# Bucketed attention and a two-layer MLP on one core: the values of batch 0 loaded once, an offset column built on TensorE, and a new table of keys

## The chip, the cores and the metric

One core of one Trainium2 chip runs the whole program; a core has TensorE (PE), VectorE (DVE), ScalarE (ACT), GpSimd (POOL) and the queue engine SyncE (SP). The metric is device microseconds of one execution, lower is better.

## The reference

Attention over four batches, eight heads, 768 rows and a head size of 64. A row of q and a row of k see each other only if six hash bits agree, the signs of their products with `proj`. The attention output, heads side by side, goes through a GELU layer pair of 512 to 2048 to 512.

```python
q_bits = (np.einsum('bhsd,dk->bhsk', q, proj) > 0)      # six bits; k likewise
mask = q_bucket[:, :, :, None] == k_bucket[:, :, None, :]
scores = np.where(mask, scale * np.matmul(q, k.transpose(0, 1, 3, 2)), -1e9)
attn = np.exp(scores - np.max(scores, axis=-1, keepdims=True))
attn = attn / (np.sum(attn, axis=-1, keepdims=True) + 1e-09)
x = np.matmul(attn, v)          # heads side by side: [3072, 512]
h = x @ w_in                    # [3072, 2048]
out = (0.5 * h * (1.0 + erf(h / sqrt(2)))) @ w_out
```

The inputs are float32. On the host the kernel's call lays q and k out as one array `qk` (128 rows by 768 per head: q above k), v as [768, 512] per batch, the weights as pairs of 32-bit words (they are decoded on the chip), and `offset`, a column of 128 numbers, in which rows 0 to 5 hold a tiny negative and rows 6 to 11 a tiny positive number, and rows 64 to 75 the same.

## The kernel before

**What runs.** The work is cut into 192 *units*: one block of 128 query rows of one head against all 768 keys. A unit (`unit`, line 892) is a score product into a PSUM tile `s` (line 908, or 910 and 911), a row maximum on DVE (L914), three small steps, an exponential on ACT (L928), a reciprocal (L937) and a division. Then the 128 by 768 probabilities are turned: in batch 0 by six PE transposes into PSUM (L987) with two copies back (tile `pt`), in the later batches by a DMA transpose after a split into two float16 halves. `values` (line 1016) multiplies them with v: L1031 with float32 values (batch 0 and the batch after it), L1040 with halves. The result `x` feeds the hidden layer (L1249), its evacuation and GELU on ACT, a split on DVE, and the output layer (L1331).

**Batch 0** is cut into two passes (`FIRST`): all eight heads for rows 0 to 255 (16 units), then all eight for the other 512 (32 units). Its heads are *plain* in the first pass (`head_plain`, line 842): q and k are loaded as they are (two loads of 64 by 768 each, L849), four small products give the hash values (L861), ACT takes their signs with `off` as bias (L866), and four copies write masks beside q and k. The bias settles the sign of a hash value of exactly zero. All other heads go through `head` (line 562): one load of 128 by 768 (`raw`, L572), its maximum on DVE (L575), a scale by way of a small product (`head_scale`, L532), a split into halves with copies and moves, hash products (L640) and signs with the bias `off16` (L646).

**Set-up** (`set_up`, line 472). `off` is loaded in four pieces on ACT's queue (L370). `off16`, which holds the column in another arrangement, is cleared (L493) and then loaded in eight small pieces on SP's queue (`offsets`, line 486, issued at L490).

**Values of batch 0.** `v_scale` (line 776) finds the largest magnitude of v: four loads of 128 by 6 by 128, one per pair of heads (L784), four maxima (L789), and a few small steps for a scale that `x` needs (L1061). For batch 0 these loads land in the buffers `wraw`, which afterwards receive the weights. The product reads v from elsewhere: `values_whole` (line 811) loads the same pieces again into the buffers `vhl` (L813), four in the first pass and four in the second.

**What sets the order.** Nothing is issued by hand. Each piece of work is a `Step` with an engine (or several that may do it), a cost and a key; `Plan.order` (line 119) goes through them as events, gives each free engine the ready step with the lowest key plus a shift for the engine, and the program is then written in that order. Every engine runs its own list strictly in that order. The keys come from the table `PAR` and the unit's number. 64 *blank* steps of four products each (L389, key 5000) fill PE wherever the planner sees nothing else to run there. Transfers from HBM all go out on SP in the planner's order.

**Weights.** Each of the 32 loads (L690, three `wraw` buffers) is decoded by three DVE operations (L697, L702, L707); a sum, a scale and three more steps per piece follow. The first hidden product needs the first pieces of `w_in` and all four values products of pass one, the first output product all of `w_out`.

Of the kernel before, what the change touches and what calls it, by code (L numbers as in the profile page):

```python
# [27 lines left out]
AGAIN = True  # L28
# [9 lines left out]
    GU_DVE=12.93, GU_Pool=23.01, SH_DVE=474.62, SH_ACT=-566.41, SH_Pool=-194.7, SF_DVE=13.82, SF_ACT=164.49,  # L38
    SF_Pool=-77.05, SU=313.06, NM_DVE=465.33, NM_ACT=-11.1, NM_Pool=261.04, NM_SP=-57.72, NL_DVE=-732.35,
    NL_Pool=-225.08, XP_ACT=-107.14, XP_DVE=-71.55, NK_DVE=262.22, NK_ACT=164.86, NK_Pool=-190.77, Z=-28.74,  # L40
    VS0=-28.69, H0=-46.77, HL=-468.9, VS=-385.02, G2=146.26, HQ=184.3, VQ=34.81, in0=-124.68, out0=147.71,
    in1=-22.23, out1=111.68, in2=5.45, out2=-184.07, in3=335.08, out3=20.9, H1=-274.68, H2=83.88, H3=-145.99,
    H4=-544.95, H5=-495.67, H6=-517.16, H7=420.16, MEV=56.34, MGE=425.93, MSP=53.47, V0=125.36, QK0=-178.02,
    QK1=77.64, QK2=-58.51, MX0=-72.3, MX1=96.72, MX2=-417.35, EX0=-69.8, EX1=-45.81, EX2=-119.6, NR0=-35.05,
    NR1=74.41, NR2=-160.33, HI0=119.84, HI1=-119.13, HI2=39.72, LO0=135.81, LO1=-111.61, LO2=-740.17, PV0=166.39,
    PV1=237.86, PV2=-124.61, TR0=10.73, TR1=-527.43, TR2=-20.06, V1=254.91, V2=-82.63, Sin0=125.72, Sin1=837.91,
    Sin2=359.76, Sin3=86.37, Sout0=124.88, Sout1=-732.71, Sout2=1.53, Sout3=-12.51, Lin=65.88, Pin=-905.87,
    Qin=627.41, Cin=450.71, Min=-117.7, Lout=-273.67, Pout=-69.41, Qout=53.69, Cout=-95, Mout=677.1, G0=55.47,
    G1=-37.8, G3=286.73, G4=139.49, G5=-122.62, G6=-350.27, G7=-70.09, DUP0=-214.64, DUP1=-22.18, DUP2=61.29,
# [27 lines left out]
class Plan:  # L77
# [16 lines left out]
    START = {"PE": 1.3, "DVE": 4.6, "Pool": 1.3, "SP": 0.7, "ACT": 3.7}  # L94
# [157 lines left out]
def tile_bucket_attention_moe(  # L252
# [103 lines left out]
    nc.sync.dma_start(out=praw[D:, :NBIT], in_=proj)  # L356
# [10 lines left out]
    off16 = const.tile([P, 1], F32, tag="off16", name="off16")  # L367
    off = const.tile([P, 1], F32, tag="off", name="off")
    for n in range(4):
        nc.scalar.dma_start(out=off[n * 32 : (n + 1) * 32], in_=offset[:32])  # L370
# [101 lines left out]
    def set_up():  # L472
# [13 lines left out]
        def offsets():  # L486
            for n in range(4):
                for m in range(2):
                    r0 = n * 32 + m * 2 * NBIT
                    nc.sync.dma_start(out=off16[r0 : r0 + 2 * NBIT], in_=offset[: 2 * NBIT])  # L490
# [932 lines left out]
```

## Time and profile before

| | us |
|---|---|
| three runs | 895.19, 900.14, 903.4 (median 900.14) |
| the profiled execution's own time | 900.27 |
| its span in the profile | 898.5 |
| granted TensorE clock, mean | 0.992 |
| PE busy | 864.0 (96%) |
| PE weight loads busy | 576.9 (64%) |
| DVE busy | 676.4 (75%) |
| ACT busy | 634.8 (71%) |
| POOL busy | 409.2 (46%) |

A row such as `L914 DVE TENSOR_REDUCE rows<-s ... x192 | 180.1, 947 | 10.4 <-PE s L911 8.9` reads: line 914, DVE, tile `rows` written from tile `s`, 192 times; 180.1 us busy, 947 ns each; 10.4 us in which DVE stood idle just before it, 8.9 of them until PE had finished line 911. In a table of stretches the columns are: the stretch, its length, then the busy time and number of instructions of PE, PEld, DVE, ACT and POOL, the granted clock (1.00 is full speed), the busy share of the DMA engines, and GB/s. In a timeline: start, duration, engine, line, operation; `x40` after a row joins 40 of a kind, and a bracket gives the idle time ahead of it and what ended it. `SPq` rows are DMA issues on SP: their duration is the time the queue took, not the transfer's.

### The profile page before, as it was taken

The page shows a single profiled execution, that of the slowest core. Times are in us where ns is not written, and L with a number is a line of the kernel's source. Part 1 is how long each engine was busy: PE and PEld are TensorE (multiplying, and loading weights), DVE is VectorE, ACT ScalarE, POOL GpSimd, SP SyncE. Part 2 cuts the span into 40 slices and gives each one's busy share as a digit, 9 for nine tenths or more (in the row PEclk, how much of TensorE's full clock was granted, in tenths as well). Part 3 has the DMA queues.
Part 4 walks back from the last instruction along what each step waited for, and adds up shares of the span by engine and source line. Part 5 has one row for each costly group of instructions (what it writes and reads, how often), then busy time and mean ns, then how long its engine had stood idle before and what let it go on. Part 6 is the DMA issues. An engine that isn't in the chain of part 4 may idle for free. (4 is left out here: it accounts for less than half of the span.)

```text
span 898.5 us, 18181 instructions
## 1 busy us (share of the span) xinstructions
PE 864.0 (96%) x6881; PEld 576.9 (64%) x6881; DVE 676.4 (75%) x1425; ACT 634.8 (71%) x1080; POOL 409.2 (46%) x480
## 2 busy tenths in 40 slices
PE   7898999998999999999999999999999999999998
PEld 4555666665666657666757657757667667576663
DVE  2899999898889899989888998988897831212122
ACT  2678997998788887898896878996986833232221
POOL 1343673967475556587775555665632400000000
PEclk8999999999999999999999999999999999999999
DMA  8775544215777989777878875888676650000000
GB/s 205 206 225 184 154 129 125 65 51 100 158 150 161 165 181 199 161 160 157 167 143 185 185 154 127 157 160 166 115 127 127 126 95 1 24 2 24 1 24 24
DMA packets 288424, 113.92 MB, mean 127 GB/s; under 512 B 229200, under 2 KB 276816, under 8 KB 288336
## 3 DMA queue, kind: packets, MB, share of 16 engines
q1 hardware_dynamic: 288064, 112.75, 58.1%
q8 instruction: 54, 0.88, 0.4%
q14 instruction: 34, 0.28, 0.1%
q10 hardware_dynamic: 272, 0.00, 0.0%
HBM read 44.31 MB, written 6.29 MB: 56 GB/s over the span
## 5 line engine op out<-in xcount | busy, mean ns | idle before, releaser
L1249 PE MATMUL hp<-x,Win 128*128 128x256 f16 x2304 | 268.2, 273 | 4.0 <-DVE x L1068 3.3
L1331 PE MATMUL hp<-Wout,g 128*128 128x512 f16 x1152 | 261.9, 379 | 0.0
L1249 PEld LDWEIGHTS <-Win 128*128 128x128 f16 x2304 | 224.7, 98 | 44.2 <-issue 7.4
L1331 PEld LDWEIGHTS <-g 128*128 128x128 f16 x1152 | 109.8, 98 | 125.8 <-issue 4.8
L914 DVE TENSOR_REDUCE rows<-s 128x1 f32<-128x768 f32 x192 | 180.1, 947 | 10.4 <-PE s L911 8.9
L928 ACT ACTIVATE p<-s,rows 128x768 f32<-128x768 f32 x143 | 141.0, 987 | 19.2 <-DVE rows L424 7.4
L1259 ACT ACTIVATE h<-hp,ffs 128x512 f32<-128x512 f32 x96 | 65.4, 681 | 99.3 <-PE hp L1249 99.0
L910 PE MATMUL s<-Q 88*128 88x384 f16 x304 | 99.6, 328 | 6.8 <-ACT wraw L928 3.2
L911 PE MATMUL s<-K 128*128 128x384 f16 x304 | 99.3, 327 | 0.0
L424 DVE TENSOR_SCALAR g<-h,ffs 128x512 f16<-128x512 f32 x31 | 15.7, 505 | 108.1 <-ACT h L1287 77.0
L943 DVE SCALAR_TENSOR_TENSOR hl<-p,rows,hl 128x768 f16<-128x768 f32 x66 | 73.0, 1109 | 6.9 <-POOL hl L424 5.9
L1040 PE MATMUL hp<-pt,vhl 128*64 128x256 f16 x1296 | 77.0, 274 | 0.2
L1301 DVE SCALAR_TENSOR_TENSOR g<-h,ffs,g 128x512 f16<-128x512 f32 x96 | 73.1, 777 | 3.0 <-POOL g L424 0.5
L1040 PEld LDWEIGHTS <-vhl 128*64 128x64 f16 x1296 | 68.7, 110 | 10.1 <-issue 9.2
L919 POOL TENSOR_SCALAR rows<-rows,hs 128x1 f32<-128x1 f32 x66 | 49.0, 743 | 54.0 <-DVE rows L914 50.7
L444 POOL TENSOR_TENSOR K<-raw,Q 64x768 f16<-64x768 f32 x40 | 68.0, 1699 | 3.3
L424 POOL TENSOR_SCALAR rows<-rows 128x1 f32<-128x1 f32 x102 | 40.8, 400 | 59.3 <-ACT p L928 37.1
L424 POOL TENSOR_SCALAR hl<-p,rows 128x768 f16<-128x768 f32 x29 | 32.0, 1102 | 45.5 <-DMA pt<-hl 19.3
L424 POOL TENSOR_SCALAR raw<-raw,hs 64x768 f32<-64x768 f32 x40 | 46.8, 1170 | 10.5 <-ACT Q L421 7.3
L928 ACT ACTIVATE wraw<-s,rows 128x768 f32<-128x768 f32 x49 | 48.3, 986 | 4.1 <-POOL rows L424 1.7
L424 POOL TENSOR_SCALAR Q<-sign 24x384 f16<-24x384 f16 (+1 forms) x57 | 34.5, 605 | 30.6 <-ACT sign L866 19.6
L911 PEld LDWEIGHTS <-K 128*128 128x128 f16 x304 | 29.9, 98 | 27.5 <-issue 10.0
(157 smaller groups left out, 1343.2 us busy)
## 6 DMA issues: line engine op xcount, KB each, us to landing
raw<-qk SPq DMA_DIRECT2D x26, 384.0 KB
vraw<-v SPq DMA_DIRECT2D x24, 384.0 KB
wraw<-w_in SPq DMA_DIRECT2D x16, 512.0 KB
wraw<-w_out SPq DMA_DIRECT2D x16, 512.0 KB
out<-o SPq DMA_DIRECT2D x11, 512.0 KB
K<-Q SPq DMA_DIRECT2D x36, 96.0 KB
vhl<-v SPq DMA_DIRECT2D x8, 384.0 KB
Q<-Q SPq DMA_DIRECT2D x20, 96.0 KB
```

The lines of the kernel that those rows point to most:

```text
L424: on.tensor_scalar(out=out, in0=in_, scalar1=scale, scalar2=bias, op0=ALU.mult, op1=ALU.add)
L444: on.tensor_tensor(out=out, in0=in0, in1=in1, op=ALU.subtract)
L910: nc.tensor.matmul(to, aq[kk, qs], ak[kk, n], start=True, stop=False)
L911: nc.tensor.matmul(to, bq[:, qs], bk[:, n], start=False, stop=True)
L914: nc.vector.tensor_reduce(out=nm, in_=both(sp), axis=AX.XY, op=ALU.max, negate=True)
L928: nc.scalar.activation(out=buf(ex).rearrange("p (b k) -> p b k", b=2), in_=both(sp), func=AF.Exp, scale=sc, bias=nb, accum_out=ssum,)
L943: nc.vector.scalar_tensor_tensor(out=buf(hi)[:, 1], in0=buf(ex), scalar=r, in1=buf(hi)[:, 0], op0=ALU.mult, op1=ALU.subtract,)
L1040: nc.tensor.matmul(pv[j * D : (j + 1) * D], buf(vh)[:, tv, kt, j * D : (j + 1) * D], buf(holds[j][0])[:, tp * KT + kt, :nt], start=kt == 0 ...
L1249: nc.tensor.matmul(buf(pair[0])[:, j * ch[1] : (j + 1) * ch[1]], win_hl[:, f0 // WB1, tw, pr, f0 % WB1 : f0 % WB1 + P], x[:, tx, pr, : ch[1]],
L1259: nc.scalar.activation(out=values_of()[:, 2 * fp : 2 * fp + 2, :nt], in_=buf(pair[0])[:, : 2 * nt].rearrange("p (j k) -> p j k", j=2), fun ...
L1301: nc.vector.scalar_tensor_tensor(out=gt[:, 1, s2, :nt], in0=h[:, s2, :nt], scalar=sg, in1=gt[:, 0, s2, :nt], op0=ALU.mult, op1=ALU.subtract,)
L1331: nc.tensor.matmul(buf(banks[u]).rearrange("p (c f) -> p c f", c=NWB), gt[:, tg, f, u * P : (u + 1) * P], wout_hl[:, :, tw, ft], start=ft ...
```

## The change

1. **Values of batch 0.** A new tile `v_first` (128 by 6 by 512, float32) in the pool that exists only until the late buffers are needed. Three loads of 128 by 2 by 512 fill it (runs of 512 elements instead of 128). Three maxima of 1024 elements each replace four of 768. The first pass's values products read `v_first`; its four loads into `vhl` are gone. The second pass still loads into `vhl`.
2. **Offset column.** One load of the whole column on ACT's queue. POOL makes `shift`, two matrices of shifted identities; two PE products put the two arrangements beside each other in PSUM; DVE copies them out as `both_offs`, of which `off` and `off16` are the two columns. The eight loads on SP and the four on ACT are gone; the second load of `proj` moves from SP to ACT. The first sign now waits for the copy.
3. **Table and planner constants.** Nearly all keys of `PAR` are new, one (`VB`) is added, and three assumed engine start times and one assumed load cost are changed. The program's order is therefore another one on every engine, from start to end. `AGAIN` changes its form, not its effect: sets with index 6 or more are dropped as before.

```diff
-AGAIN = True
+AGAIN = 6
-    GU_DVE=12.93, GU_Pool=23.01, SH_DVE=474.62, SH_ACT=-566.41, SH_Pool=-194.7, SF_DVE=13.82, SF_ACT=164.49,
+    VB=-40.97, GU_DVE=240.54, GU_Pool=100.45, SH_DVE=167.52, SH_ACT=204, SH_Pool=-19.66, SF_DVE=464.07,
...
-    START = {"PE": 1.3, "DVE": 4.6, "Pool": 1.3, "SP": 0.7, "ACT": 3.7}
+    START = {"PE": 1.1, "DVE": 4.2, "Pool": 1.3, "SP": 0.7, "ACT": 2.7}
...
+    v_first = early.tile([P, KT, NPAIR * P], F32, tag="v_first", name="v_first")
...
-    nc.sync.dma_start(out=praw[D:, :NBIT], in_=proj)
+    nc.scalar.dma_start(out=praw[D:, :NBIT], in_=proj)
+    offs = const.tile([P, 1], F32, tag="offs", name="offs")
+    nc.scalar.dma_start(out=offs, in_=offset)
...
-    for n in range(4):
-        nc.scalar.dma_start(out=off[n * 32 : (n + 1) * 32], in_=offset[:32])
...
-        def offsets():
-            for n in range(4):
-                for m in range(2):
-                    r0 = n * 32 + m * 2 * NBIT
-                    nc.sync.dma_start(out=off16[r0 : r0 + 2 * NBIT], in_=offset[: 2 * NBIT])
+        def copies():
+            src = ident
+            for n, by in ((0, 2 * (D // 4)), (1, 2 * NBIT), (1, 2 * NBIT + D // 2)):
+                nc.gpsimd.affine_select(
+                    out=shift[:, n], in_=src, compare_op=ALU.not_equal, fill=1.0, base=by, pattern=[[-1, P]],
+                    channel_multiplier=1,
+                )
+                src = shift[:, n]
+        def spread():
+            for n in range(2):
+                nc.tensor.matmul(buf(sp)[:, n : n + 1], shift[:, n], offs16, start=True, stop=True)
+        def take():
+            nc.vector.tensor_copy(out=both_offs, in_=buf(sp)[:, :2])
...
-        sg = add("ACT", 0.1 + 0.833e-3 * HS + 0.186, sign, key + PAR[f"PRJ{cl}"], [pp])
+        sg = add("ACT", 0.1 + 0.833e-3 * HS + 0.186, sign, key + PAR[f"PRJ{cl}"], [pp, offs_ready])
...
+        def load_rows(k):
+            nc.sync.dma_start(
+                out=v_first[:, 2 * k : 2 * k + 2], in_=v[b].rearrange("(c p) d -> p c d", p=P)[:, 2 * k : 2 * k + 2]
+            )
+        def biggest_rows(k):
+            nc.vector.tensor_reduce(
+                out=stat_v[:, b, k : k + 1], in_=v_first[:, 2 * k : 2 * k + 2], axis=AX.XY, op=ALU.max,
+                apply_absolute_value=True,
+            )
...
-                vhl = values_whole(b, pr, key) if whole else values_halves(b, pr, key, v_ready[b])
+                if n_pass == 0:
+                    assert whole
+                    vhl = (first_v[-1], None)
+                else:
+                    vhl = values_whole(b, pr, key) if whole else values_halves(b, pr, key, v_ready[b])
```

**How the order moves.** Three places, each as the built program lists it (a line number, an operation, the tile written and its source, the size; the numbers of the lines differ between the two programs).

SP's list at the start. The Q and K pairs, `x_107` with `x_108`, and `x_109` with `rest` are the q and k tiles of plain heads; the pair 88 and 89 belongs to head 0, the pair 90 and 91 to head 1. Before, rows 8 to 19 (ahead of them stand `proj`, two pairs of q and k, and two loads of v into `vhl`):

```order
L849 DMA Q_88<-qk 64x768
L849 DMA K_89<-qk 64x768
L849 DMA Q_94<-qk 64x768
L849 DMA K_95<-qk 64x768
L784 DMA wraw_82<-v 128x6x128
L784 DMA wraw_83<-v 128x6x128
L784 DMA wraw_84<-v 128x6x128
L849 DMA Q_90<-qk 64x768
L849 DMA K_91<-qk 64x768
L572 DMA raw_77<-qk 128x768
L572 DMA raw_78<-qk 128x768
L490 DMA off_133<-offset 12x1 x8
```

The change, rows 8 to 19 (ahead of them `x_107`, `x_108`, `raw_77` and the pairs 88 and 92):

```order
L881 DMA Q_90<-qk 64x768
L881 DMA K_91<-qk 64x768
L588 DMA raw_78<-qk 128x768
L881 DMA Q_94<-qk 64x768
L881 DMA K_95<-qk 64x768
L881 DMA Q_115<-qk 64x768
L881 DMA K_116<-qk 64x768
L706 DMA wraw_82<-w_in 128x2x512
L706 DMA wraw_83<-w_in 128x2x512
L810 DMA v_first<-v 128x2x512 x3
L881 DMA x_109<-qk 64x768
L881 DMA rest<-qk 64x768
```

The pair of head 1 and `raw_78` move ahead of all values; two pieces of `w_in` now go before them, where before the first stands at row 25.

DVE's list from the maxima of units 1 and 2 (both of head 0) to that of unit 3 (head 1). Before, the last rows of that stretch:

```order
L806 TENSOR_REDUCE tiny<-stat_v 128x1
L937 RECIPROCAL rows<-rows 128x1
L547 RECIPROCAL hs<-hs 128x1
L424 TENSOR_SCALAR diag_87<-ident,tiny 128x128
L424 TENSOR_SCALAR rows<-rows 128x1
L547 RECIPROCAL hs<-hs 128x1
L937 RECIPROCAL rows<-rows 128x1
L424 TENSOR_SCALAR x_109<-sign_71 12x384
L914 TENSOR_REDUCE rows<-s_61 128x1
L697 TENSOR_SCALAR Win<-wraw_83 128x512
```

The change:

```order
L713 TENSOR_SCALAR Win<-wraw_83 128x512
L723 SCALAR_TENSOR_TENSOR Win<-wraw_82,Win 128x512
L969 RECIPROCAL rows<-rows 128x1
L427 TENSOR_SCALAR K_91<-sign_71 12x384
L815 TENSOR_REDUCE stat_v<-v_first 128x1
L718 SCALAR_TENSOR_TENSOR Win<-wraw_83,Win 128x512
L969 RECIPROCAL rows<-rows 128x1
L815 TENSOR_REDUCE stat_v<-v_first 128x1
L723 SCALAR_TENSOR_TENSOR Win<-wraw_83,Win 128x512
L427 TENSOR_SCALAR Q_94<-sign_71 12x384
L815 TENSOR_REDUCE stat_v<-v_first 128x1
L946 TENSOR_REDUCE rows<-s_61 128x1
```

The decoding of two pieces of `w_in` has moved ahead of unit 3's maximum, and all three maxima of `v_first` stand directly ahead of it.

PE's list around the first scores (units 1 and 2, head 0). Before:

```order
L861 MATMUL hp_63<-Q_94,hash_139 32x384
L861 MATMUL hp_63<-K_95,hash_139 32x384
L908 MATMUL s_61<-K_89,Q_88 128x384 x2
L908 MATMUL s_62<-K_89,Q_88 128x384 x2
L861 MATMUL hp_66<-Q_90,hash_139 32x384
L861 MATMUL hp_66<-K_91,hash_139 32x384
```

The change:

```order
L548 LDWEIGHTS twin
L548 MATMUL hp_66<-tops,twin 128x1
L940 MATMUL s_61<-K_89,Q_88 128x384 x2
L940 MATMUL s_62<-K_89,Q_88 128x384 x2
L893 MATMUL hp_63<-Q_90,hash_139 32x384
L893 MATMUL hp_63<-K_91,hash_139 32x384
```

The small product for the scale of the second `raw` head (L548) now stands directly ahead of the first scores; it needs the maximum of `raw_78`. Behind the products of the pair 90 and 91, the change has 84 blank products, six transposes, the four products of the pair 94, and then unit 3's scores.

More of the change, by code (lines that the diff above doesn't have):

```diff
@@ L366, in tile_bucket_attention_moe @@
     hash16 = const.tile([P, 2, 32], F16, tag="hash16", name="hash16")
[L367 to L370 removed]
+    offs16 = const.tile([P, 1], BF16, tag="offs16", name="offs16")
+    both_offs = const.tile([P, 2], F32, tag="both_offs", name="both_offs")
+    off, off16 = both_offs[:, :1], both_offs[:, 1:]
+    shift = const.tile([P, 2, P], BF16, tag="shift", name="shift")
     hash32 = const.tile([D, 32], F32, tag="hash32", name="hash32")
@@ L501, in set_up @@
         a = add("Pool", 1.4, sums, key, [])
-        z = add("DVE", 0.1, clear, key, [])
-        o = add("SP", 0.5, offsets, key, [z])
+        c = add("Pool", 0.9, copies, -1000.0, [])
+        z = add("DVE", 0.07, narrow, -1000.0, [])
+        sp = add("PE", 0.2, spread, -1000.0, [c, z], takes="hp")
+        o = add("DVE", 0.07, take, -1000.0, [sp])
+        free(sp, [o])
         m = add("DVE", 0.1, largest, key, [])
@@ L523, in set_up @@
         hi = add("DVE", 0.2, high, key, [sc])
-        return [add("DVE", 0.2, low, key, [hi]), o]
+        return [add("DVE", 0.2, low, key, [hi])], o
     def head_scale(top, w, key, needs, n):
@@ L779, in raw @@
         def raw(step):
[L780 to L781 removed]
+            return buf(step)
         def load(pr, box):
@@ L792, in biggest @@
             )
+        def load_rows(k):
[7 more added lines that the diff above has]
+            )
         parts = []
-        for pr in range(NPAIR):
+        for k in range(KT // 2 if b == 0 else 0):
+            first_v.append(add("SP", 1.8, lambda k=k: load_rows(k), key))
+            parts.append(add("DVE", 1.14, lambda k=k: biggest_rows(k), key + PAR["VB"], first_v[-1:]))
+        for pr in range(NPAIR if b else 0):
             box = []
-            box.append(
-                add("SP", 1.43, lambda pr=pr, box=box: load(pr, box), key, takes="wraw" if b == 0 else "vraw")
-            )
+            box.append(add("SP", 1.43, lambda pr=pr, box=box: load(pr, box), key, takes="vraw"))
             parts.append(add("DVE", 0.87, lambda pr=pr, box=box: biggest(pr, box), key, [box[0]]))
@@ L812, in load, with whole_of @@
         def load():
-            nc.sync.dma_start(out=whole_of(raw), in_=v[b, :, words(pr)].rearrange("(c p) d -> p c d", p=P))
+            nc.sync.dma_start(out=whole_of(raw, pr), in_=v[b, :, words(pr)].rearrange("(c p) d -> p c d", p=P))
         raw = add("SP", 1.43, load, key - PAR["VQ"], takes="vhl")
         return raw, raw
-    def whole_of(step):
+    def whole_of(step, pr):
+        if step is first_v[-1]:
+            return v_first[:, :, words(pr)]
         return buf(step).rearrange("p t c d -> p (t c d)").bitcast(F32).rearrange("p (c d) -> p c d", c=KT)
@@ L849, in load @@
                 nc.sync.dma_start(out=both_of[k][:D], in_=qk[b, h][k * D : (k + 1) * D])
-            loads.append(add("SP", 0.75, load, key - PAR["HQ"], clear))
+            loads.append(add("SP", 0.92, load, key - PAR["HQ"], clear))
         space = add("none", 0, lambda: None, key, loads, takes="sign")
@@ L868, in head_plain @@
         pp = add("PE", 0.75, project, key + PAR[f"PRJ{cl}"], [space], takes="hp", table="quarter", act=0.5)
-        sg = add("ACT", 0.1 + 0.833e-3 * HS + 0.186, sign, key + PAR[f"PRJ{cl}"], [pp])
+        sg = add("ACT", 0.1 + 0.833e-3 * HS + 0.186, sign, key + PAR[f"PRJ{cl}"], [pp, offs_ready])
         free(pp, [sg])
@@ L1049, in values @@
             add(
-                "PE", (2.74 if whole else 2.05) * nt / TC, product, key, [vh, vl, xt[b, ch], *turns],
+                "PE", (2.74 if whole else 2.05) * nt / TC, product, key, [*(first_v if vl is None else (vh, vl)), xt[b, ch], *turns],
                 takes="hp", table="half",
```

58 lines of the change are left out of this document (31 added, 27 removed).

## Prediction

> **What bounds the kernel now.** I read the page's busy shares first, then the table of stretches. Columns are as explained above the diff.
>
> ```profile
> PE 864.0 (96%) x6881; PEld 576.9 (64%) x6881; DVE 676.4 (75%) x1425; ACT 634.8 (71%) x1080; POOL 409.2 (46%) x480
> ```
>
> ```profile
> 0.00:35.00 35.00, 26.13 (x218) 16.26 (x219) 13.83 (x44) 12.02 (x20) 7.48 (x25) 0.90 0.80 190
> 35.00:212.00 177.00, 163.40 (x1258) 110.76 (x1257) 166.62 (x400) 155.70 (x291) 103.18 (x119) 0.99 0.49 138
> 212.00:225.00 13.00, 12.16 (x78) 8.20 (x78) 10.19 (x24) 9.97 (x19) 8.23 (x5) 0.87 0.61 117
> 225.00:740.00 515.00, 507.57 (x4272) 338.84 (x4272) 451.05 (x904) 416.88 (x706) 290.27 (x333) 1.00 0.77 154
> 740.00:899.00 159.00, 154.75 (x1064) 102.80 (x1058) 34.72 (x55) 40.20 (x46) 0.00 (x0) 1.00 0.04 14
> ```
>
> PE bounds the kernel from 225 us on: 507.57 of 515 and 154.75 of 159 us, and most of the last gap is the tail. There a change of order can win little. Before 225 it is otherwise. From 35 to 225, DVE is busy 166.62 + 10.19 = 176.8 of 190 us (93%), PE partly with blanks, so DVE sets the pace. In the first 35 us nothing is full: DVE works 13.8 us, and 12.9 of PE's 26.1 us are blanks:
>
> ```profile
> 0.00:35.00 35.00, 12.90 (x148) 11.70 (x148) 0.90 0.80 190
> ```
>
> The start therefore waits for data. The timelines of SP, PE and DVE show which.
>
> ```profile
> 0.73 0.60 SPq L356 DMA_DIRECT2D praw<-proj  x1
> 1.38 0.74 SPq L849 DMA_DIRECT2D Q<-qk  x1
> 7.81 4.81 SPq L784 DMA_DIRECT2D wraw<-v  x3
> 13.94 3.52 SPq L849 DMA_DIRECT2D Q<-qk  x1
> 19.65 6.58 SPq L490 DMA_DIRECT2D off<-offset  x8
> ```
>
> ```profile
> 14.29 1.35 PE L861 MATMUL hp<-Q,hash 64*32 64x384 f32 x2 [3.13 <-DMA Q<-qk]
> 15.40 0.84 PE L861 MATMUL hp<-K,hash 64*32 64x384 f32 x1
> 16.84 4.45 PE L389 MATMUL hp<-blank 128*128 128x128 bf16 x40
> 22.42 2.82 PE L908 MATMUL s<-K,Q 76*128 76x384 f32 x8 [0.34 <-DVE K L424]
> 26.04 1.72 PE L389 MATMUL hp<-blank 128*128 128x128 bf16 x28
> ```
>
> ```profile
> 24.98 0.95 DVE L575 TENSOR_REDUCE tops<-raw 128x1 bf16<-128x768 f32 x1 [1.20 <-DMA raw<-qk]
> 34.73 0.96 DVE L914 TENSOR_REDUCE rows<-s 128x1 f32<-128x768 f32 x1
> 35.88 0.43 DVE L697 TENSOR_SCALAR Win<-wraw 128x512 int32<-128x512 int32 x1 [0.19 <-DMA wraw<-w_in]
> ```
>
> Head 0's q and k land at 14.29 and 15.40, behind two loads of v; the first scores start at 22.42; unit 3's maximum, the first of head 1, at 34.73; the first piece of `w_in` lands at 35.88. The eight tiny offset loads hold SP's queue for 6.58 us, with all of `w_in` behind them.
>
> **The change, step by step.** My measure is when DVE reaches unit 3's maximum, and what PE and DVE then have behind them at unit 57, which before falls at about 225 us, where PE takes over.
>
> *Landing.* A q or k tile has 0.197 MB, a `raw` or an old piece of v 0.393, a piece of `w_in` or of `v_first` 0.524. Counted from SP's first load at 1.38, `raw_77` came after 4.33 MB at 24.98: 0.183 MB/us. The first `w_in` came after 6.42 MB at 35.88; without the 6.58 us of the stalled queue that is 0.230. The worst is K of head 0: 1.97 MB at 15.40, 0.140. In the new order the last piece of `v_first` ends 5.77 MB, and SP starts with it at 0.73, since `proj` has left its queue. It lands at 32.2 (0.183), 28.9 (0.205, the middle, which I take) or 25.8 (0.230). For the upper rate speaks that short runs go:
>
> ```profile
> 10.00:15.00 5.00, 1.87 (x22) 1.12 (x20) 0.40 (x2) 1.62 (x3) 0.67 (x1) 0.95 1.10 211
> 15.00:20.00 5.00, 5.00 (x37) 3.36 (x37) 0.95 (x1) 1.62 (x3) 0.51 (x1) 0.50 0.84 207
> 30.00:35.00 5.00, 3.97 (x21) 1.90 (x19) 2.85 (x13) 1.85 (x4) 1.34 (x2) 1.00 1.07 272
> 35.00:40.00 5.00, 4.74 (x38) 2.87 (x37) 4.81 (x10) 4.09 (x9) 3.08 (x8) 1.00 1.08 300
> ```
>
> While the runs of 128 elements came in, 207 to 211 GB/s moved; with longer ones 272 to 300. A page of the Trainium skill speaks against this: "DMA: Bandwidth & Descriptors", section Specifications, puts full rate at pieces of 512 bytes and more, and a run of 128 float32 is just that. By that rule longer runs win nothing, the rate stays at 0.183, and the sum below would end 3.3 us later, near 896; these four rows look the other way, but other things changed between them too.
>
> *Unit 3's maximum.* On DVE it stands behind the maximum of that last piece, 1024 elements: 953 ns x 1024/768 = 1.27 us. So 28.9 + 1.3 = 30.2. PE must not be later: `raw_78` ends 2.36 MB, lands at 12.2; its maximum 0.95 and the small product 0.5 give 13.7; two units of scores 2.82, the four products up to the blanks at 26.04 about 0.8: 17.3; then 84 blanks at 1.72/28 = 61 ns are 5.2 (at the 111 ns of the row at 16.84 they are 9.3): 22.5; transposes and four products 1.8, scores 1.4: 25.7, slow 29.8. DVE is the later one. **Term 1: 34.73 - 30.2 = -4.5 us** (ends: -1.2 and -7.6).
>
> *DVE work.* Ahead of unit 3 now stand two whole decodings:
>
> ```profile
> L702 DVE SCALAR_TENSOR_TENSOR Win<-wraw,Win 128x512 int32<-128x512 int32 x16 | 10.8, 680 | 0.0
> L707 DVE SCALAR_TENSOR_TENSOR Win<-wraw,Win 128x512 int32<-128x512 int32 x16 | 11.2, 710 | 0.0
> L697 DVE TENSOR_SCALAR Win<-wraw 128x512 int32<-128x512 int32 x16 | 7.8, 488 | 2.0 <-DMA wraw<-w_in 1.9
> L789 DVE TENSOR_REDUCE stat_v<-wraw 128x1 f32<-128x768 f32 x4 | 3.8, 953 | 11.1 <-DMA wraw<-v 11.0
> L424 DVE TENSOR_SCALAR pt<-hp 128x384 f32<-128x384 f32 x28 | 14.8, 547 | 1.2 <-PE hp L987 1.1
> ```
>
> 2 x (0.488 + 0.680 + 0.710) = 3.8 us; 1.3 us of small rows have gone behind it; the maxima of v weigh the same (3 x 1.27 against 4 x 0.95). 2.5 us are ahead of time. All rows of DVE with their means add up to 760 us, where the engine was busy 676 (operations overlap), so I count 0.89: **Term 2: -2.2.** Ahead of unit 57 the new list has 4.7 us more of rows than the old one, mostly seven more copies to `pt` (3.8) that ACT had: **Term 3: 0.89 x 4.7 = +4.2.** The ends: if ACT's relief counts, 0; if the rows do not overlap, 4.7.
>
> *PE at unit 57.* Ahead of its scores the old list has 168 hidden products, 12 output products and 32 hash products of later heads, the new one 192, 18 and 40. From the chain of waits:
>
> ```profile
> 643.91 1.31 PE hp L1249 x12
> 647.85 1.29 PE hp L1331 x6
> 649.14 0.44 PE hp L640 x8
> ```
>
> 24/12 x 1.31 + 1.29 + 0.44 = 4.4 us that PE need not do later: **Term 4: -4.4.** It runs in gaps that the first stages have (35 - 26.13 and 177 - 163.40, 22 us of idle up to 212). If the gaps do not fall where these products stand, it is worth 0.
>
> *The wait at 212.* Before, PE stood idle for a PSUM buffer behind the last float32 values product:
>
> ```profile
> 212.84 2.72 PE L1249 MATMUL hp<-x,Win 128*128 128x256 f16 x12 [2.93 <-DVE x L1068]
> ```
>
> One unit of scores lay between. Now eight hash products, six output products and two units lie there, some 2.2 us more. DVE idled 13 - 10.19 = 2.8 us in that stretch; I take a little under half, **Term 5: -1.2** (ends 0 and -2.8).
>
> *After 225.* Two units of scores with nothing between them need both `s` buffers; behind unit 57 the old list has 21 such pairs, the new one 25. The waits from 225 to 740:
>
> ```profile
> PE s L910 <- ACT p L928: 2.6, 5, 1.3
> PE s L910 <- ACT wraw L928: 2.1, 2, 1.7
> ```
>
> 4.7/21 x 4 = **Term 6: +0.9.**
>
> *At nothing.* The offset column: the load, three selects of about 0.3 us on POOL, two tiny PE products and two DVE copies. All are done by about 7 us; the first scores wait for `raw_78` until 12.2, which covers them. Without that cover the signs would set the start, and a late column would cost its lateness. That v of batch 0 comes once (1.57 MB) in place of twice in the first pass is part of Term 1, through what stands ahead of each load. The 256 blanks are as many as before.
>
> Sum: -4.5 - 2.2 + 4.2 - 4.4 - 1.2 + 0.9 = -7.2. From the profiled execution's own 900.27 (0.13 above the median of the runs) that gives **893 us**, 0.8% faster. One per cent is about what a measurement of this kernel can tell from no change, so this is "same" by a little. With the ends of Terms 1, 4 and 5 the forecast alone spans 888 to 898.
>
> **The rivals.**
>
> *More than that.* Data comes at 0.230, Term 1 is -7.6, and PE's wait at 212 goes wholly, -2.8: -7.6 - 2.2 + 4.2 - 4.4 - 2.8 + 0.9 = -11.9, **888 us**; if starting full also closes a quarter of DVE's 13.2 idle us between 35 and 225, 885. For it: the rows at 30 to 40 us. Against it: PE must reach unit 3 by 27.1, and does so only if its clock stays up; after the 3.13 us of idle before 14.29 the row from 15 to 20 shows a clock of 0.50. The Trainium skill ("TensorE: Matmul & The Clock Gate", Part 1: The HAM clock gate) says the same of an idle window of about 3.4 us; by it a wait for `raw_78` of that length makes the blanks slow, PE comes at 29.8, and this rival shrinks to the forecast. The trace agrees, one drop in five-microsecond slices.
>
> *The values come too late (slower).* DVE executes in order, and every score maximum from unit 3 on stands behind three maxima of `v_first`, whose loads stand behind all but two heads and behind 1.05 MB of weights. At the 0.140 that head 0 saw, the last piece lands at 41.9 and unit 3 is reached at 43.2: Term 1 is +8.5, the sum +5.8, **906 us**. It decides from a landing at 36.1 on (sum zero), a rate of 0.163. For it: the early rates. Against it: they were measured behind short runs and with SP's queue full.
>
> *The paired scores wait.* If each of the 25 pairs waits as the seven that waited did, 4.7/7 = 0.67, Term 6 is 25 x 0.67 - 4.7 = +12.0 and the sum +3.9: **904 us**. Against it: two thirds of the old pairs waited not at all.
>
> **How the numbers follow.** Forecast (893): 0.50. More: 0.24. Values late: 0.14. Pairs: 0.12. Faster by over 1% means below 891.1: nearly all of the second case and a third of the forecast's span, 0.40. Slower by over 1%, above 909: the far end of the last two, 0.08. Within: 0.52. The range takes in the second case and most of the two slow ones: 884 to 905.
>
> **What would show it.** Right: the three `v_first` maxima end by about 30, unit 3's maximum directly behind; the first scores at 13 to 15 in place of 22.4; no 6.58 us hole on SP; the stretch to PE's last idle shorter by 6 or 7 us. Wrong: unit 3's maximum after 34, DVE below 93% in the stage behind it, idle on PE ahead of L942 well above 5 us after the stage, or the first scores waiting for `both_offs`.

## The result and the profile after

The change is slower: 910.43 us in the median of six runs (905.23 to 913.0) against 899.6 of the kernel before; the ratio is 1.0117, 95% interval 1.0078 to 1.0156. The forecast was 893. The profiled execution of the change took 905.23 (span 903.4), the fastest of the six; a second profile of it (e5 below) took 913.28 (span 911.5), so the main readings from the one are checked in the other.

The busy shares and the table of stretches of the change, in the columns of before:

```profile
PE 870.2 (96%) x6883; PEld 581.0 (64%) x6883; DVE 686.4 (76%) x1402; ACT 638.8 (71%) x1098; POOL 434.5 (48%) x509
```

```profile
0.00:35.00 35.00, 30.55 (x282) 21.27 (x283) 20.49 (x53) 16.08 (x30) 8.98 (x28) 1.00 0.98 233
35.00:212.00 177.00, 161.08 (x1157) 108.39 (x1156) 166.72 (x384) 145.76 (x267) 99.20 (x117) 0.95 0.38 112
212.00:225.00 13.00, 13.00 (x107) 8.72 (x105) 11.51 (x25) 10.34 (x21) 9.67 (x8) 1.00 0.77 141
225.00:740.00 515.00, 505.75 (x4218) 336.01 (x4217) 452.25 (x887) 424.00 (x735) 316.63 (x357) 1.00 0.78 152
740.00:904.00 164.00, 159.82 (x1126) 106.60 (x1124) 35.40 (x57) 42.60 (x49) 0.00 (x0) 1.00 0.05 17
```

The start is fuller, as forecast: DVE works 20.5 of the first 35 us instead of 13.8. Then look at 35 to 212. DVE is busy 166.72 us, within 0.1 us of the 166.62 of before, in 384 instructions instead of 400; PE has done 1157 instructions instead of 1258, and its clock is 0.95 instead of 0.99. DVE has 23 rows less in the whole program and 10 us more of busy time. A busy engine that gets less done: that is where to look.

The start itself, timeline of DVE in the change:

```profile
25.45 1.22 DVE L815 TENSOR_REDUCE stat_v<-v_first 128x1 f32<-128x1024 f32 x1
27.82 1.22 DVE L815 TENSOR_REDUCE stat_v<-v_first 128x1 f32<-128x1024 f32 x1 [0.48 <-DMA v_first<-v]
30.60 1.22 DVE L815 TENSOR_REDUCE stat_v<-v_first 128x1 f32<-128x1024 f32 x1
31.73 0.95 DVE L946 TENSOR_REDUCE rows<-s 128x1 f32<-128x768 f32 x1
```

Unit 3's maximum stands directly behind the third maximum of `v_first`, as the prediction had it, at 31.73 instead of 34.73. (The last piece landed at 29.7, forecast 28.9; its maximum began 0.9 us later, behind two rows that DVE's list puts first.) I followed the start times of this row through the program (rows of L914 and L946, in order): the change leads by 10.3 us at unit 12 (58.40 against 68.69) and 4.9 at unit 17, is about level from unit 22 to 25 (2.0 ahead to 1.5 behind), and is 6.1 behind at unit 57:

```profile
227.24 0.95 DVE L914 TENSOR_REDUCE rows<-s 128x1 f32<-128x768 f32 x1
```

```profile
233.31 1.81 DVE L946 TENSOR_REDUCE rows<-s 128x1 f32<-128x768 f32 x2
```

(The second joins units 57 and 58.) In between, grouping DVE's rows by form from unit 3 to unit 58, the rows add up to about 208 us before and 218 in the change: some 4 us of that are other or more rows, some 6 are the same forms taking longer. One place shows how. Timelines of DVE, POOL and PE of the change:

```profile
125.85 2.38 DVE L723 SCALAR_TENSOR_TENSOR Wout<-wraw,Wout 128x512 int32<-128x512 int32 x1
128.15 0.54 DVE L427 TENSOR_SCALAR pt<-hp 128x384 f32<-128x384 f32 x1
128.62 0.14 DVE L551 TENSOR_SCALAR hs<-hp 128x2 int32<-128x2 int32 x1
128.69 0.54 DVE L427 TENSOR_SCALAR pt<-hp 128x384 f32<-128x384 f32 x1
...
129.45 2.14 DVE L713 TENSOR_SCALAR Wout<-wraw 128x512 int32<-128x512 int32 x1
```

```profile
125.55 2.13 POOL L447 TENSOR_TENSOR Win<-o,Win 128x1024 f16<-128x1024 f32 x1
127.78 1.43 POOL L427 TENSOR_SCALAR o<-Win,tiny 128x1024 f32<-128x1024 f32 x1
129.18 2.12 POOL L447 TENSOR_TENSOR Win<-o,Win 128x1024 f16<-128x1024 f32 x1
```

```profile
126.25 0.19 PE L548 MATMUL hp<-tops,twin 128*128 128x1 bf16 x2
128.75 1.00 PE L736 MATMUL hp<-Wout 128*64 128x64 bf16 x16 [2.30 <-DVE pt L427]
129.68 5.49 PE L940 MATMUL s<-K,Q 76*128 76x384 f32 x8
```

L723 usually takes 0.68 us, L713 0.42. Started just after POOL's subtraction of the weights' low half, they take 2.38 and 2.14, and end 0.55 and 0.29 us after POOL's instruction (127.68 and 131.30). The copy to `pt` behind the first is late, PE waits 2.30 us for the buffer it frees, and the eight score products behind take 5.49 us where others take 2.85. The window 120 to 140 us, of the change:

```profile
120.00:140.00 20.00, 17.21 (x113) 11.75 (x112) 16.48 (x43) 14.20 (x25) 11.47 (x15) 0.74 0.35 94
```

Clock 0.74, and now DVE has 3.5 us of idle too, for it waits for the slow scores. The second profile has the same 0.74 there.

The other place, at 198 us, has the same first link. A conversion that DVE does once, 0.75 us long where POOL's subtraction is cut (e14 below), stands beside a whole subtraction; the copies to `pt` wait behind it, and PE waits 2.19 us for them:

```profile
198.12 2.21 DVE L427 TENSOR_SCALAR Wout<-o 128x1024 f16<-128x1024 f32 x1
```

```profile
197.65 2.13 POOL L447 TENSOR_TENSOR Wout<-o,Wout 128x1024 f16<-128x1024 f32 x1
```

```profile
200.97 4.23 PE L1063 MATMUL hp<-pt,vhl 128*64 128x256 f32 x22 [2.19 <-DVE pt L427]
```

To size the stretched rows I summed, over DVE's rows between units 3 and 58, what each takes beyond the tenth percentile of its form where that is over 0.2 us: 10.8 us before, 16.6 in the change (16.9 in its second profile); below this is the stretched sum. The conversion at 198 us, the only one of its form, is not in it. 9.5 us of the 16.6 lie for about half their length or more beside POOL's subtractions for the weights, 6.0 of the 10.8. Both kernels have twelve of these subtractions on POOL: what differs is what DVE does beside them. The Trainium skill describes the cause ("SBUF — State Buffer", section Who interferes with whom): a DVE instruction of certain kinds and a GpSimd instruction share a pair of ports, which is an exclusive lock for the whole instruction, so that the later one stands still. The rows agree: in the change five decoding rows start behind a subtraction of POOL, and all five end 0.28, 0.29 or 0.55 us behind it; they hold 8.7 of the 9.5 us.

### The profile page after: what moved, and what is told of

Read it like the earlier page. It is cut to its first block, busy times and chain, and to the rows that moved or that the text cites. A ratio compares the mean times of both kernels' runs of the same rounds, so it can differ in the third digit from the quotient of the medians.

```text
span 903.4 us, 18142 instructions
## 1 busy us (share of the span) xinstructions
PE 870.2 (96%) x6883; PEld 581.0 (64%) x6883; DVE 686.4 (76%) x1402; ACT 638.8 (71%) x1098; POOL 434.5 (48%) x509
## 4 chain that ended last, share of the span: by engine, by line
PE 48%; DVE 8%; ACT 6%; DMA 4%; issue 2%; POOL 1%; SPq 0%; ACTq 0%; POOLq 0%; DVEq 0%
PE hp L1370 19%; PE hp L1288 18%; PE hp L1072 4%; PE s L942 3%; DMA pt<-hl 3%; PE s L943 3%; DVE rows L946 2%; DVE hl L975 2%; ACT p L960 2%; DMA vraw<-v 1%; ACT Q L424 1%; ACT wraw L960 1%; DVE g L1340 1%; DVE wraw L975 1%; ACT hl L424 1%
## 5 line engine op out<-in xcount | busy, mean ns | idle before, releaser
L946 DVE TENSOR_REDUCE rows<-s 128x1 f32<-128x768 f32 x192 | 179.5, 947 | 8.5 <-PE s L943 4.6
L942 PE MATMUL s<-Q 88*128 88x384 f16 x304 | 99.3, 327 | 8.8 <-ACT p L960 7.2
L427 POOL TENSOR_SCALAR rows<-rows 128x1 f32<-128x1 f32 x111 | 48.6, 437 | 63.9 <-ACT p L960 41.9
L1340 DVE SCALAR_TENSOR_TENSOR g<-h,ffs,g 128x512 f16<-128x512 f32 x96 | 76.1, 806 | 2.8 <-DVE g L427 0.5
L447 POOL TENSOR_TENSOR K<-raw,Q 64x768 f16<-64x768 f32 x42 | 72.7, 1730 | 3.5
L975 DVE SCALAR_TENSOR_TENSOR hl<-p,rows,hl 128x768 f16<-128x768 f32 x54 | 57.7, 1071 | 5.7 <-ACT hl L424 3.0
L943 PEld LDWEIGHTS <-K 128*128 128x128 f16 x304 | 29.8, 98 | 30.2 <-issue 14.0
L975 DVE SCALAR_TENSOR_TENSOR wraw<-p,rows,wraw 128x768 f16<-128x768 f32 x42 | 45.8, 1090 | 4.1 <-POOL wraw L427 4.0
L940 PE MATMUL s<-K,Q 76*128 76x384 f32 x112 | 44.2, 527 | 3.7 <-ACT p L960 3.5
```

The costliest lines, as they stand in the source:

```text
L427: on.tensor_scalar(out=out, in0=in_, scalar1=scale, scalar2=bias, op0=ALU.mult, op1=ALU.add)
L447: on.tensor_tensor(out=out, in0=in0, in1=in1, op=ALU.subtract)
L942: nc.tensor.matmul(to, aq[kk, qs], ak[kk, n], start=True, stop=False)
L943: nc.tensor.matmul(to, bq[:, qs], bk[:, n], start=False, stop=True)
L946: nc.vector.tensor_reduce(out=nm, in_=both(sp), axis=AX.XY, op=ALU.max, negate=True)
L975: nc.vector.scalar_tensor_tensor(out=buf(hi)[:, 1], in0=buf(ex), scalar=r, in1=buf(hi)[:, 0], op0=ALU.mult, op1=ALU.subtract,)
```

## The experiments

**Theory A**: the loss lies between 35 and 235 us; the new order brings DVE's decoding rows beside POOL's subtractions, and DVE sets the pace. **Theory B**: the new code itself costs. **Theory C**: PE's waits and its clock carry it. **Theory D**: the extra copies to `pt`. In most kernels the order is kept as the planner wrote it, and only what a step issues is altered.

**e1 and e2: keys and code apart.** The code of the change with the old table (the change's `VB`, assumed engine starts and load cost stay), and the old code with the new table, starts and load cost.

```diff
# e1, in the change          # e2, in the kernel before
-    VB=-40.97, GU_DVE=240.54, ...      -    GU_DVE=12.93, ...
+    VB=-40.97, GU_DVE=12.93, ...       +    GU_DVE=240.54, ...
```

> The changed code (values of batch 0 once, offset column by a product) with the old table of keys, VB as in the change; the assumed engine starts and the assumed load cost stay those of the change. Theory A (the start gains, and the new order of DVE and POOL gives it back between 35 and 235 us): unit 3's maximum at 32 or earlier, DVE stretched beside POOL by less than the 16.6 us of the change in that stage, total 893 to 902. Theory B (the new code itself costs: longer values maxima ahead of unit 3, v_first held by all loads): total 907 or more, unit 3 not ahead of 31.7.

> The old code with the new table of keys, assumed starts and assumed load cost. Theory A: the loss is in the order, so without the new code's earlier start it is slower than the change, 912 or more. Theory B: about the time of before, 898 to 903.

Measured: e1 931.8 us, ratio to before 1.0356 (1.0293 to 1.0420); e2 942.0, 1.0472 (1.0408 to 1.0537). Both are far slower than either kernel. By their letter e1 meets Theory B (907 or more) and e2 Theory A (912 or more), but losses of 32 and 43 us can't be parts of one of 11, so neither theory is separated: each table is worth something only with the code that it goes with. For the rest the order is kept, and none of those runs tests Theory B by itself.

**e3 and e4: POOL's subtractions only cleared**, in the change and in the kernel before.

```diff
             def low(dst=dst, box=box):
+                if box[2].engine == "Pool":
+                    nc.gpsimd.memset(dst[:, 1], 0.0)
+                    return
                 subtract(
```

> The change, with the weights' low halves that POOL computes (a subtraction of two operands, about 2.1 us) only cleared instead; this leaves out that part of the weights. Order unchanged. Theory A (DVE stands still while POOL subtracts, and DVE sets the pace up to 235 us): the rows of DVE that took 1.5 to 2 us too long beside these subtractions (9.5 us in sum) go back to their usual length, the maximum of unit 57 comes at 224 to 228 instead of 233.3, total 897 to 902 (8 to 13 below the change's median of 910.4). Theory C (PE and its clock set the pace, DVE's long rows are incidental): 908 to 912.

> The kernel before, with the same part left out: weights' low halves on POOL only cleared. Theory A: 6.0 us of DVE's stretched rows go away, total 893 to 897. Theory C: within 2 us of before, 898 to 902.

Measured: e3 899.42, ratio 1.0020 (0.9994 to 1.0046), 11 us below the change's median, or 8 to 9 us by the ratios; e4 896.75, 0.9990 (0.9951 to 1.0029). The change loses about 1% to these subtractions, the old order nothing that can be told apart. In e3's profile the stretched sum is about 10 us instead of 16.6. In total Theory A holds, with a gain about the size of the 9.5 us of the rows. One part of its forecast missed: unit 57 came at 229.63 and not at 224 to 228, in a profile that is the slowest of e3's ten runs. Clearing is also shorter than subtracting, so e3 alone leaves open whether POOL's own time counts; the runs with pieces below keep all of the work.

**e5 to e8: four runs on the change.** e5 is the change itself. e6 moves seven copies, e7 adds blanks where PE waits, e8 cuts every subtraction on POOL in four.

```diff
# e6, behind steps = plan.order(); is_copy marks the copies to pt
+    moved = [s for s in steps if hasattr(s, "is_copy") and s.engine == "DVE"]
+    for n in (14, 15, 18, 19, 20, 33, 34):
+        moved[n].engine = "ACT"
# e7; fill issues n blank products
+FILL = {720: 34, 1109: 18}
         for n, s in enumerate(steps):
+            if n in FILL:
+                fill(FILL[n], bufs["s"][0][:, 0, S // 2 : BANK] if n == 720 else buf(s)[:, :P])
             s.emit()
# e8, in subtract
-        on.tensor_tensor(out=out, in0=in0, in1=in1, op=ALU.subtract)
+        parts = 4 if engine == "Pool" else 1
+        w = out.shape[1] // parts
+        for n in range(parts):
+            c = slice(n * w, (n + 1) * w)
+            on.tensor_tensor(out=out[:, c], in0=in0[:, c], in1=in1[:, c], op=ALU.subtract)
```

> The changed kernel once more, nothing altered, beside the three variants that follow on the same chip. All theories: 906 to 913.

> The change with its order kept, but seven of the 35 copies to pt that its keys give to DVE are done by ACT at the same place (the 15th, 16th, 19th to 21st, 34th and 35th). Theory D (DVE's extra copies, term 3 of the prediction, are what costs): DVE is relieved of 3.8 us and PE's 2.3 us wait for a copy at 126 us goes away, total 4 to 6 us below the change. Theory A (the collisions with POOL carry the loss): at most 3 us below, DVE's stretched rows between 35 and 235 us stay near 16 us.

> The change with its order kept, plus 34 blank products ahead of the product of Wout at which PE waited 2.3 us at 126 us and 18 ahead of the float32 values product at 198 us, so that PE does not stand still there. Theory C (the dropping clock carries the loss): the scores behind the first place take 2.9 us again instead of 5.5, the clock of 120 to 140 us is 0.95 or more instead of 0.74, total 3 to 6 us below the change. Theory A: the rows get shorter, but DVE sets the pace there, total within 2 us of the change.

> The change with its order kept, but each subtraction on POOL (weights and K, 2.1 and 1.7 us) is issued as four of a quarter of the width. Nothing is left out. Theory A: DVE waits for a quarter at most, stretched rows between 32 and 234 us fall from 16.6 to 9 to 12 us, total 3 to 7 us below the change. Theory C: within 2 us of the change, or up to 2 us slower for POOL's extra instructions.

Measured: e5 908.99, ratio 1.0104 (1.0051 to 1.0157); e6 904.4, 1.0049 (1.0020 to 1.0079); e7 901.07, 1.0001 (0.9972 to 1.0030); e8 909.0, 1.0101 (1.0060 to 1.0142).

e7 speaks against Theory A alone: most of DVE's rows stay long, and yet 8 us are gone, more than the 3 to 6 of Theory C. Its timeline of PE, where L1428 are the added blanks:

```profile
127.98 2.06 PE L1428 MATMUL s<-blank 128*128 128x128 bf16 x34
130.36 0.67 PE L737 MATMUL hp<-Wout 128*64 128x64 bf16 x16 [0.32 <-DVE pt L428]
130.96 2.85 PE L941 MATMUL s<-K,Q 76*128 76x384 f32 x8
```

and of DVE:

```profile
127.45 2.39 DVE L724 SCALAR_TENSOR_TENSOR Wout<-wraw,Wout 128x512 int32<-128x512 int32 x1
```

The collision is there, PE comes no earlier to its product, but it stays at full clock: 0.67 instead of 1.00, 2.85 instead of 5.49 us. So the two theories are one chain: collision, late copy, idle PE, half clock, late scores, late DVE. e6 fits Theory D's number, but in it the wait at 126 us shrinks to 1.25 us and the clock stays at full speed there, so its gain need not be DVE's relief; see e10.

e8 missed. It does in the stage what Theory A says (stretched sum 10.1 us, unit 57 at 226.04 instead of 233.31), and loses it later, where only K's subtractions are left and have become longer: behind 234 us they take 90.8 us instead of 61.1, POOL is busy 330.92 us between 234 and 740 where the change has 310.95, and from unit 57 to the end it takes 681.8 us instead of 670.1 (676.7 in the change's second profile). The two rows, e8 and the change:

```profile
234.00:740.00 506.00, 489.64 (x4102) 326.54 (x4101) 435.63 (x849) 409.05 (x708) 330.92 (x449) 1.00 0.77 148
```

```profile
234.00:740.00 506.00, 497.48 (x4157) 330.93 (x4156) 444.03 (x868) 416.19 (x720) 310.95 (x350) 1.00 0.78 152
```

**e9 to e12.** e9 keeps only e7's first place, e10 moves only the two copies at 126 us, e11 has e7's blanks and cuts the weights' subtractions alone, e12 delays the start.

```diff
# e9
+FILL = {720: 34}
# e10
+    for n in (14, 15):
+        moved[n].engine = "ACT"
# e11: e7's edit, and in low
-                subtract(box[2].engine, dst[:, 1], ..., dst[:, 0])
+                parts = 4 if box[2].engine == "Pool" else 1
+                for m in range(parts):
+                    c = slice(m * n // parts, (m + 1) * n // parts)
+                    subtract(box[2].engine, dst[:, 1, c], ...[:, c], dst[:, 0, c])
# e12, in load_rows; late is a part of Wout, which is written later
+            if k == 0:
+                nc.sync.dma_start(out=late, in_=v[1].rearrange("(c p) d -> p c d", p=P)[:, :2])
```

> The change with its order kept, plus 34 blank products ahead of the product of Wout at 126 us alone. Theory C1 (one wait of 2.3 us there, and the clock that drops behind it, carry most of the loss): 901 to 904, nearly all of what the blanks at both places brought (8 us). Theory C2 (both places count alike): 904 to 907.

> The change with its order kept, but only the 15th and 16th of DVE's copies to pt, the two that PE waited for at 126 us, are done by ACT, which stands idle there for 1.4 us. It takes away the wait itself where the blanks only bridged it. Theory C1: the wait of 2.3 us and the clock's drop at 120 to 140 us are gone, 899 to 904. Theory A (DVE's lost time counts wherever it lies): DVE is relieved of 1.1 us only, 907 to 910.

> The change with its order kept, the blanks at both places, and POOL's subtractions for the weights alone in four pieces each (K's stay whole). Theory: the two add, since the pieces shortened the stage up to 234 us by 7 us and lost it later where K's subtractions had become longer: 895 to 900, below the kernel before. Rival: the pieces bring nothing on top, 900 to 903.

> The change with one more load of 0.524 MB (a part of v that nothing reads) ahead of the three loads of v_first, order kept. The step of the prediction that the start counts one for one: unit 3's maximum at 33.5 to 35, 2.5 to 3 us later than the change's 30.3 to 31.7, total 2 to 4 us above the change, 911 to 914. Rival (the order falls out of step anyway, so the start does not reach the end): within 1.5 us of the change, 907.5 to 910.5.

Measured: e9 905.54, ratio 1.0081 (1.0047 to 1.0116); e10 905.71, 1.0076 (1.0047 to 1.0105); e11 897.28, 0.9978 (0.9957 to 0.9999); e12 906.96, 1.0087 (1.0061 to 1.0114).

C1 falls: the one place at 126 us, bridged or taken away, is worth 3 to 4 us by the medians, within the intervals of the change; only both places together (e7) lie clearly below. e10's 905.71 lies in neither of its forecasts; it moves two of e6's seven copies and comes within 1.3 us of e6. e11 is the change with its collisions at the weights cut short and with e7's blanks: 13 us below the change, and a little below the kernel before. e12 tells little: unit 3 came at 32.19, and in the twelve profiles of kernels with the change's start it lies anywhere from 29.19 to 32.10, so that one profile doesn't show whether the load delayed it.

**e13 to e16.** The pieces of e11 alone in the kernel before (e13) and in the change (e14); e15 is e14 with e10's edit and the blanks at 198 us; e16 is e11 with two loads more ahead of `v_first`.

```diff
# e15
+FILL = {1109: 18}
# e16, in load_rows; late as in e12, another part for each n
+            for n in (1, 2) if k == 0 else ():
+                nc.sync.dma_start(out=late, in_=v[n].rearrange("(c p) d -> p c d", p=P)[:, :2])
```

> The kernel before with its order kept and POOL's subtractions for the weights in four pieces each. Theory E (the old order is in step with the chip, its planned exclusions of DVE and POOL mostly hold): 1 to 3 us below before, 897 to 899. Rival (the pieces help any order alike): 6 us or more below, 894 or less, and the change with pieces and blanks is then no better than the old kernel with pieces.

> The change with its order kept and the weights' subtractions on POOL in four pieces, no blanks added. If the collisions are the first cause and the clock only follows: 896 to 900, near the 897.3 with blanks, with the clock of 120 to 140 us near 1.00. If the blanks carry a share of their own: 901 to 905.

> The change with the weights' subtractions in pieces, the two copies at 126 us on ACT, and 18 blanks only at 198 us. If removing the wait adds to the pieces: 893 to 896, below the kernel before by more than the measurement is uncertain. If the pieces have already taken that wait away: 896 to 899.

> The version with pieces and blanks (897.3) with two more loads of 0.524 MB ahead of v_first that nothing reads. Theory (with the order in step the start counts one for one): unit 3's maximum 3 to 5 us later, total 900 to 902. Rival (the start is not on the path in this order either): within 1.5 us, 896 to 899.

Measured: e13 897.59, ratio 0.9957 (0.9930 to 0.9983); e14 899.55, 0.9998 (0.9976 to 1.0020); e15 901.37, 1.0017 (0.9996 to 1.0037); e16 900.0, 1.0000 (0.9978 to 1.0022).

By the medians the pieces take 11 us from the change and 3 from the kernel before, so that 8 of the 10.8 us between the two kernels are the weights' subtractions on POOL, with what follows from them. By the ratios, each to the kernel before beside it, it is 9.5 to 10.7 and 3.9, so 6 to 7; the intervals leave some 5 us either way. e14 and e8 differ only in K's subtractions, and e8 is 9 us slower: that is what cutting these cost. e14 shows the chain broken at its first link, timelines of PE and DVE:

```profile
125.28 0.67 PE L736 MATMUL hp<-Wout 128*64 128x64 bf16 x16 [0.94 <-DVE pt L427]
125.88 2.85 PE L943 MATMUL s<-K,Q 76*128 76x384 f32 x8
```

```profile
29.74 0.95 DVE L949 TENSOR_REDUCE rows<-s 128x1 f32<-128x768 f32 x1
...
224.00 1.81 DVE L949 TENSOR_REDUCE rows<-s 128x1 f32<-128x768 f32 x2
```

A wait of 0.94 us leaves the clock up, and it is 1.00 from 120 to 140 us, as e14's forecast had it; unit 57 comes at 224.0 (223.2 in e11). e15 missed: the wait that e10 took away was already short, and the copies on ACT did not help. e16 is undecided too: unit 3 came at 31.25, inside that spread, and the times overlap (2.7 us by the medians).

**e17 and e18.** e17 is e13 with blanks where the kernel before stood still for 2.93 us; e18 is e11 with two small steps per unit on DVE instead of POOL, behind unit 57.

```diff
# e17, in the kernel before
+FILL = {1196: 40}
             s.emit()
+            if n in FILL:
+                fill(FILL[n], buf(s)[:, P : 2 * P])
# e18; gu.unit = sh.unit = t
+    for s in steps:
+        if getattr(s, "unit", 0) > 57 and s.engine == "Pool":
+            s.engine = "DVE"
```

> The kernel before in its order, POOL's subtractions for the weights in four pieces each, and 40 blank products behind the small product at 209.7 us, where PE stood still for 2.93 us before the hidden product. If the clock's drop there (2.72 us for twelve products instead of 1.4, the scores behind it 0.52 instead of 0.33) costs the end its length: 895 to 896.5. If DVE sets the pace there: 897 to 898.5, as with the pieces alone (897.6).

> The change with pieces and blanks (897.3), and for the units behind 57 the two small steps between the score maximum and the exponential go from POOL (0.67 and 0.46 us each) to DVE (about 0.2 and 0.15) at the same places. Theory F (the score buffers come free late because the exponential waits for POOL's small steps): PE's waits for score buffers from 234 to 740 us fall from 4.5 to 2 us or less, total 893 to 896. Rival (DVE's own list is what is late there): 896 to 900.

Measured: e17 892.75, ratio 0.9936 (0.9901 to 0.9970), the fastest of all, below both kernels; e18 905.68, 1.0075 (1.0050 to 1.0101). e17 is below both of its forecasts. Its interval still overlaps e13's, and in e13's profile the wait of 2.93 us is already down to 1.41, with the clock up behind it, so what the blanks did is not shown. The two profiles also differ by 3.9 us at unit 12, where the programs are the same. e18 is above both of its forecasts. Theory F falls: with the steps on DVE, PE's waits of 234 to 740 us grow, now for DVE. From its waits:

```profile
PE hp L1077 <- DVE hs L552: 2.4, 2, 1.9
PE hp L1293 <- DVE rows L428: 2.2, 1, 2.2
PE hp L1293 <- DVE x L1105: 0.9, 2, 0.4
```

## Why the prediction was wrong

**Term 1** was right in mechanism and in where it ends, and counted from a late start. Forecast for unit 3's maximum was 30.2; the twelve profiles with the change's start have 30.5 on average. But the 34.73 of before was the latest of the four profiles with the old start that I now have (31.35, 32.48, 32.80 in the others), 32.8 on average: typically -2.3 us, not -4.5. That the start counts one for one was not shown, since in e12 and e16 it can't be told from that spread.

**Terms 2 and 3** count rows at the mean lengths of before. The sum puts unit 57 at 227.24 - 4.5 - 2.2 + 4.2 = 224.7, and with POOL's subtractions in pieces it comes at 224.0 and 223.2. That the two agree is luck in part: the 227.24 has a late start and the collisions of before in it, and with the same pieces the kernel before reaches unit 57 at 225.34 and 222.29 (e13, e17), so between the two orders hardly anything of the forecast 2.5 us is left. In the change it comes at 233.31 and 234.84. **This is the step that failed: the mean length of a DVE row was taken as a property of the row.** It is a property of the row and of what POOL does beside it. L713 on `Win` (L697 in the kernel before, 488 ns there), in the change:

```profile
L713 DVE TENSOR_SCALAR Win<-wraw 128x512 int32<-128x512 int32 x16 | 10.9, 686 | 1.1 <-DMA wraw<-w_in 1.1
```

The trace of before held the warning: 10.8 us of stretched rows, with single rows of 1.87 us beside rows of 0.42. DVE and POOL in the kernel before:

```profile
131.96 1.87 DVE L697 TENSOR_SCALAR Wout<-wraw 128x512 int32<-128x512 int32 x1
```

```profile
131.42 2.13 POOL L444 TENSOR_TENSOR Win<-o,Win 128x1024 f16<-128x1024 f32 x1 [0.33 <-ACT Win L421]
```

I read means, and did not ask which pairs of rows the new order would set beside each other. The kernel's own source held it too: `Plan.order` keeps POOL's steps and the DVE steps marked `port`, the decodings among them, apart in the plan (`PORT`, `held`). On the chip they meet all the same; where its times leave the plan's, no run here shows. None of my rivals had this mechanism.

My test for "wrong" failed with it. I had named DVE below 93% busy behind unit 3; it is 94% (166.72 + 11.51 of 190 us). A row that stands still counts as busy. Of the other signs, idle ahead of L942 well above 5 us did show in the second profile (10.0 us, 6.2 in the first; see Term 6).

**Term 5** was a wait that moved, and its cause was misread. The 2.93 us of before, from 209.91 to 212.84, also stand behind a collision, a DVE row of 2.85 us beside a subtraction of POOL:

```profile
208.68 2.85 DVE L943 SCALAR_TENSOR_TENSOR hl<-p,rows,hl 128x768 f16<-128x768 f32 x1
```

```profile
208.59 2.13 POOL L444 TENSOR_TENSOR Wout<-o,Wout 128x1024 f16<-128x1024 f32 x1
```

With the pieces alone (e13) that row takes 1.21 us and the wait 1.41. In the change PE has no such wait there (13.00 of 13 us busy from 212 to 225), but waits for copies on DVE behind two other collisions: at 126 us, and at 198. The waits of PE in the change, 31.7 to 234.2 us:

```profile
PE hp L1063 <- DVE pt L427: 4.2, 3, 2.2
PE s L940 <- ACT p L960: 3.9, 5, 1.4
PE hp L736 <- DVE pt L427: 2.3, 1, 2.3
```

I had costed the seven copies on DVE as rows, 3.8 us, and not as something that PE waits for. What the copies cost by themselves is not shown: e6 is 4.6 us below the change by the medians, but the intervals overlap, and on top of the pieces moving two of them gained nothing (e15).

**Terms 4 and 6.** From unit 57 to the end of the span it takes 671.3 us before. Terms 4 to 6 say 4.7 less, 666.6. Measured: 670.1 in the change, 676.7 in its second profile, 672.6 in e14, 669.3 in e11. Of the 4.7 us forecast 1.2 arrive in the first profile and none in the second: what the products done ahead should have saved hardly shows at the end. Part of it is Term 6, the waits for score buffers from 225 us on, forecast at 4.7 + 0.9 = 5.6 us; the change from 234 us on:

```profile
PE s L942 <- ACT p L960: 5.2, 10, 1.2
PE s L942 <- ACT wraw L960: 1.0, 3, 0.5
```

6.2 us here, but 10.0 in the second profile: 0.6 of the 3.5 us that this stretch is too long, and 4.4 of 10.1. The rest of it stays open. Why the exponential is late is not settled; e18 excludes only that moving POOL's small steps to DVE cures it.

**The rivals.** "The values come too late" gave 906, nearly the number measured, by a mechanism that did not happen: unit 3 came at 31.7, not at 43. "The paired scores wait" is +1.5 us in the first profile (6.2 against 4.7) and +5.3 in the second, of its +12.0. The offset column held no score up, as said, though it was ready at 9.5 us and not at about 7, and the first sign waited for it: the first scores started at 17.56, 4.9 us earlier than before though later than the 13 to 15 that I gave, and 0.7 us behind `raw_78`'s maximum, which ended at 16.85.

Of the 17.4 us between forecast and median (893 to 910.4) the late arrival at unit 57 is 8.6 to 10.1 by the two profiles, the rest of the way 3.5 to 10.1 (their sums, 12.1 and 20.2 us, are the two profiled times less 893). The arrival is the failed step, with what follows from it; the cause of the rest is open.

## What to carry to other kernels

Ahead of a change of order, list the pairs of engines that can hold each other up, and take for each row the length it has alone and the length it has beside the other; a mean hides both, and a busy share counts the standing still. Cut a long instruction of the engine that blocks into pieces before moving anything, but only where the other engine is the pace (e14 gained 11 us, e8 with K's pieces lost 9 of them again). Where PE must wait some 2 us, a few dozen products without a purpose can be cheaper than the idle time (e7, 8 us).

## What the hardware showed that I had not expected

A decoding row of 0.42 us took up to 2.37 beside a subtraction of 2.1 us on POOL, while score maxima were not touched: the sixteen that lay beside such a subtraction in the two kernels (L914 and L946) took 937 to 958 ns, and 947 is the mean of all. A wait of PE of 2.30 us dropped the clock for the products behind it (5.49 us for 2.85), one of 0.94 did not; the Trainium skill ("TensorE: Matmul & The Clock Gate", Part 1: The HAM clock gate) speaks of an idle window of about 3.4 us, and here less than that was enough. There is no sharp border in these runs: a wait of 1.96 us was followed by half clock in e14 (at 188.6 us), and the same wait in e11 (at 188.9) was not. The start of one and the same code is not fixed: unit 3's maximum lay between 29.19 and 32.10 us in twelve profiles, and one or two added loads of 0.524 MB, 2.6 us each at the rate of the prediction, left it at the edge of that spread or within it (32.19 and 31.25).
